# Attention units in a fused attention and mixture kernel: the softmax normalisation of one unit issued behind the maximum of the next

## The chip, the cores and the metric

The kernel runs on one core of a Trainium2 chip. The core has five engines that work side by side, each with its own queue in program order: TensorE (PE, matrix products; PEld is its loading of weights), VectorE (DVE), ScalarE (ACT), GpSimd (POOL) and SyncE (SP), whose queue issues the DMA transfers. Engines wait for one another through semaphores. The metric is the device time of one execution in microseconds, as a median of runs.

## What is computed

Three layers follow each other. The first is attention in chunks over 4 x 8 heads, 768 positions and 64 channels, the second a gated layer of 512 to 2048 to 512, the third eight dense experts weighted by a Sinkhorn balanced gate:

```python
scores = scale * np.matmul(q_c, k_full.transpose(0, 1, 3, 2))
scores = scores - np.max(scores, axis=-1, keepdims=True)
a = np.exp(scores)
a = a / (np.sum(a, axis=-1, keepdims=True) + 1e-09)
out[:, :, c_start:c_end] = np.matmul(a, v_full)
...
h = x @ w_in
g = h * np.clip(h + 3.0, 0.0, 6.0) / 6.0
x = g @ w_out
...
for e in range(E):
    h = np.maximum(x @ w1[e], 0.0)
    out += P[:, e:e + 1] * (h @ w2[e])
```

## The kernel before

Products run in three passes of TensorE: each operand is held as a high and a low part, and high x high, high x low and low x high are added up (`passes`, L230 to L232). ScalarE makes the high part by a copy (`hh`, `xh`), VectorE the low part by a subtraction (`hl`, `xl`).

The attention is cut into 32 units of 96 queries by 8 heads. A unit goes through these steps: its scores (`a_scores`, L286, one bank of PSUM for each half of the heads); the mask added while the scores are taken out of PSUM (L297), the maximum of each row and head (L305) and its negated, scaled copy `nm` (L310), all three on VectorE in `a_max`; eight exponentials on ScalarE, one for each head, which also sum the rows (`a_exp`, L322); the normalisation on VectorE in `a_norm`, with the tiny addition to the sum `sm` (L330), the reciprocal `rc` (L332) and the multiplication (L333); eight transposes on TensorE into `pt` (`a_turn`, L340) and two copies of these by ScalarE into `et` (`a_copy`, L168); and the product with the values, `av` (`a_values`, L360). Its result is split into parts `xh` and `xl`, and GpSimd adds these to `xf`, which is stored for the residual of later layers (`a_whole`, L384).

The second layer runs in the same loop over `steps`. A step makes one product of 128 hidden rows by 384 tokens (`layer_product`, 12 matmuls into `ph`), the bias and relu on ScalarE (L430, tile `t`), the gate's product on VectorE (L435), the two parts, and two steps later the second product into `pa` (`second`, 12 matmuls). From the 17th step on, every odd step ("due") carries the parts of three units: the values of unit u, the normalisation of unit u + 1, the scores, maximum and exponentials of unit u + 2. The even step behind it carries the transposes of unit u + 1. The code's order in a step is the order in each engine's queue: the kernel is written under a manual schedule. On ScalarE the order from one due step on is: exponentials of u + 2, relu of the even step, `et` copies of u + 1, then the next due step.

Beside this run two streams of work. Weights come as wide integers and are converted on ScalarE and VectorE (L148 to L161). And a "factory" on GpSimd makes sums and differences of expert weights for the third layer: 80 jobs, each a load, four additions (tile `fr`, L717) and a store, paced by the number of the step.

Of the kernel before, what the change touches and what calls it, by code (L numbers as in the profile page):

```python
# [67 lines left out]
def attn_moe_moe(ctx: ExitStack, tc: tile.TileContext, qk, vw, wi, wo, wa, wb, wg, out):  # L68
# [10 lines left out]
    def pool(name, bufs, space=None, side=None):  # L79
        kw = {} if space is None else {"space": space}  # L80
        if side:
            kw["side"] = side
        return tc.tile_pool(name=name, bufs=bufs, reuse_waits="tile", **kw)
# [40 lines left out]
    def w_load(f):  # L124
        for t in "ab":
            s = wst[1, f, t] = st_p.tile([128, DM], F32, tag=f"s{t}", name=f"s{t}")
            nc.sync.dma_start(out=s, in_=wd[t, f])
# [18 lines left out]
    def single_act(n):  # L146
        rest = at_p.tile([128, DM], U32, tag="rest", name="rest", bufs=3)
        nc.scalar.activation(out=rest, in_=words(n)[0], func=AF.Copy, scale=7.49 * 2.0 ** -32)  # L148
        pw = at_p.tile([128, DM], F32, tag="pw", name="pw", bufs=3)
        nc.scalar.activation(out=pw, in_=words(n)[1].bitcast(F32), func=AF.Abs, scale=2.0 ** -112)  # L150
        wst[n] = pw, rest
# [20 lines left out]
    def single_hi(n, eng=nc.scalar):  # L172

        pe, f, t = wide[n]
        if pe == 0:
            hi = w_p.tile([128, DM], F32R, tag=f"w{t}h", name=f"w{t}h")
            copy(hi, wst[n], eng)
            wts[t, pe, f] = hi
# [26 lines left out]
    def convert_act(n):  # L205

        for m in range(going[0], min(going[0] + n, len(wide))):
            single_act(m)
        for m in range(going[1], going[0]):
            single_hi(m)  # L210
        going[1] = going[0]
# [192 lines left out]
    def stage(do, u):  # L404
        if u < NU:
            do(u)
# [31 lines left out]
    def first(i):  # L438
        layer_product(i)
        layer_relu(i)  # L440
        layer_times(i)
# [32 lines left out]
    def spill():  # L474
        while spills:
            nc.sync.dma_start(out=spills[0][0], in_=spills.pop(0)[1])
# [375 lines left out]
    def w1_load(g):  # L852
        if g < NW:
            n, k, p = W1[g]
            e = n % NE
            s = w1s[g] = w1s_p.tile([128, 2, 256], F32, tag="w1s", name="w1s", bufs=4)
            wk = wa[4 * e:4 * e + 4].rearrange("k p (a f) -> p k a f", a=4)
            if k in FORM and p in (1, 2):
                for j in range(2):
                    nc.sync.dma_start(out=s[:, j].rearrange("p (k f) -> p k f", k=2),  # L860
                                      in_=quarter((ws3 if k == DEEP else ws4)[e], W3S[S1 + 2 * p - 2 + j]))
            elif k in FORM:
                q = wk[:, :, (A12 if k == DEEP else A22) + 1].rearrange("p k (j f) -> p j k f", j=2)
                for j in range(2 if p == 0 else 1):
                    nc.sync.dma_start(out=s[:, j].rearrange("p (k f) -> p k f", k=2),
                                      in_=q[:, j, :2] if p == 0 else q[:, 1, 2:])
            elif FIRST[p][0] < S1:
                nc.sync.dma_start(out=s, in_=wk[:, k:k + 2, FIRST[p][0] + 1])
            else:
                nc.sync.dma_start(out=s, in_=ws1[2 * e + k // 2][:, W1S[FIRST[p][0]]])  # L870
# [10 lines left out]
    def w1_hi(g):  # L881
        if g < NW:
            w1[g] = w1_p_tile("h")
            nc.scalar.activation(out=w1_part(g, w1[g]), in_=w1_part(g, w1s[g]), func=AF.Copy)  # L884

    def w1_lo(g):
        if g < NW and w1_low(g)[1]:
            lo = w1_p_tile("l")
            nc.vector.tensor_tensor(out=w1_part(g, lo), in0=w1_part(g, w1s.pop(g)),
                                    in1=w1_part(g, w1[g]).bitcast(F32), op=ALU.subtract)  # L890
            w1[g] = w1[g], lo
        elif g < NW:
            w1[g] = w1[g], w1l.pop(g)
# [13 lines left out]
    def w2_load(m):  # L907
        if m < 7 * NM:
            e, a = m // 7 % NE, SECOND[m % 7][0]
            s = w2s[m] = w2s_p.tile([128, 4, 256], F32, tag="w2s", name="w2s")  # L910
            if a >= S1:
                nc.sync.dma_start(out=s, in_=ws2[e][:, W2S[a]])
                return
            for g in range(2):
                of = wb[e, g].rearrange("p (c a d) -> p c a d", c=2, a=4)[:, :, {A11: 0, A12: 2, A22: 3}[a]]
                nc.sync.dma_start(out=s[:, 2 * g:2 * g + 2], in_=of)
# [242 lines left out]
    with tc.manual_schedule():  # L1159
# [10 lines left out]
        def rate(i):  # L1170

            pe, b, f = steps[i]
            return 0 if pe or b == NB1 - 1 else f % 2
# [6 lines left out]
        def sums_due(i):  # L1180
            now = i if i <= NB1 * NF else NB1 * NF + (i - NB1 * NF) * PACE
            for stage_, late in ((2, 2.6), (0, 0), (1, 1.3)):
                while begun[stage_] < len(jobs) and starts[begun[stage_]] + late <= now:
                    jobs[begun[stage_]][stage_]()
                    begun[stage_] += 1

        for i, (pe, b, f) in enumerate(steps):
            if i < 2 * NF:
                continue
            u, turn, due = (i - 2 * NF) // 2 + 3 * UPB, i % 2 == 0, i % 2 == 1  # L1190
            turn, due = (pe == 0 and w for w in (turn, due))
            if (pe, b, f) == (0, NB1 - 1, 0):
                at_ctx.__exit__(None, None, None)
            if (pe, b, f) == (1, 1, 0):
                three.close()
                xo_p = ctx.enter_context(pool("xo", 1, side="right"))
                xb_p = xb_ctx.enter_context(pool("xb", 1, side="right"))
            if (pe, b, f) == (1, NB2 - 1, 2):
                assert build is None and begun[2] == len(jobs)
                xb_ctx.close()  # L1200
                two.close()
                w1s_p, w1r_p, w2s_p = (
                    ctx.enter_context(pool(n, 1, side="right")) for n in ("w1s", "w1r", "w2s"))
                for g in range(4):
                    w1_load(g)
                w2_load(0)
            if (pe, b) == (1, NB2 - 1) and 3 <= f <= AHEAD + 2:
                w1_hi(f - 3)
                w1_lo(f - 3)
                if f < AHEAD + 2:  # L1210
                    w1_load(f + 1)

            sums_due(i)
            if pe == 0 and b == NB1 - 1:
                w_load(f)
                if f == 0:
                    x_load(0)
            if pe == 1 and f == 1 and b + 1 < NB2:
                x_load(b + 1)
            if pe == 1 and f == 5:  # L1220
                x2_load(b)
            ready = pe == 1 and f == 3 and later
            spill()
            first(i)
            if pe or due:
                first_parts(i)
            if due:
                stage(a_values, u)
                stage(a_split, u)
                stage(a_norm, u + 1)  # L1230
                stage(a_scores, u + 2)
                stage(a_max, u + 2)
                convert_act(rate(i))
                stage(v_load, u + 2)
            if ready:
                gate_logits(later[0])
                gate_copy(later[0])
            second(i - LAG)
            if ready:
                gate_turn(later.pop(0))  # L1240
            if pe:
                sums_due(i + 0.5)
            if due:
                stage(a_exp, u + 2)
                stage(a_load, u + 4)
            if pe == 0 and not due:
                if turn:
                    stage(a_transpose, u)
                first_parts(i)
                convert_act(rate(i))  # L1250
            if pe == 0:
                convert(rate(i))
            if pe == 0 and b == NB1 - 1 and f >= LAG:
                w_split(f - LAG)
            elif pe == 1 and b == 0 and f < LAG:
                w_split(NF - LAG + f)

            n = b + 1 if pe else 0
            r = f - 2 - pe
            if 0 <= r < KT and n < NB2 and (pe or b == NB1 - 1):  # L1260
                x_split(n, r)
            if (pe, b, f) == (1, 2, 6):
                build = x_ops(0, xb_p, "xb")
            if build:
                build = build if next(build, 0) is None else None
# [228 lines left out]
```

## Time and profile before

| | us |
|---|---|
| median of 3 runs (2518.59 to 2521.33) | 2519.56 |
| the profiled execution | 2521.98 |
| its span, first to last instruction | 2519.9 |
| TensorE busy in the span | 2484.1 (99%) |
| VectorE busy | 1995.3 (79%) |
| ScalarE busy | 1445.8 (57%) |
| GpSimd busy | 947.5 (38%) |

The due steps that the change touches lie between about 128 and 356 us of the span. The list of waits names a waiting engine and line, and the engine and line that ended the wait. A timeline row gives start, length, engine, line, and in brackets how long the engine had stood idle before it and what released it. Matmuls overlap: one that is listed with 0.34 us may begin 0.17 us behind the one before it.

### The profile page before, as it was taken

The numbers are of one execution on the slowest core, as the hardware profiler recorded it, in microseconds if no ns is written. First come the engines' busy times: TensorE is split into PE (matmuls) and PEld (weight loads), VectorE is DVE, ScalarE is ACT, GpSimd is POOL, SyncE is SP. The second block draws the span as 40 slices with busy tenths as digits, with TensorE's granted clock in tenths as the row PEclk, the third lists the DMA queues.
The fourth block names the chain that finished last, engine by engine and source line by source line (L and its number), as shares of the span: only waits on it lengthen the run. The fifth ranks groups of instructions, "written<-read, shape, count | busy, mean of one in ns | idle before, by whom it ended". The sixth has DMA issues, their size and how long they took to land. (4 is left out here: it accounts for less than half of the span.)

```text
span 2519.9 us, 37015 instructions
## 1 busy us (share of the span) xinstructions
PE 2484.1 (99%) x13092; PEld 2125.0 (84%) x13092; DVE 1995.3 (79%) x2440; ACT 1445.8 (57%) x2686; POOL 947.5 (38%) x705
## 2 busy tenths in 40 slices
PE   9989999999999999999999999999999999999999
PEld 8988889878778888888888888888888888888888
DVE  8777757567489999999997787778788677777777
ACT  8656654122265655565666655566666666656555
POOL 0154556666006535344533233333233222232231
PEclk9999999999999999999999999999999999999999
DMA  7679969887465676676768777667777667776664
GB/s 208 195 241 294 286 214 317 276 302 252 143 224 173 221 235 226 223 240 198 242 223 281 253 246 241 221 232 235 240 254 243 225 226 230 234 230 205 216 220 157
DMA packets 379990, 587.45 MB, mean 233 GB/s; under 512 B 30675, under 2 KB 229276, under 8 KB 379804
## 3 DMA queue, kind: packets, MB, share of 16 engines
q1 hardware_dynamic: 379520, 584.85, 71.3%
q8 instruction: 103, 1.69, 0.3%
q14 instruction: 83, 0.68, 0.1%
q10 hardware_dynamic: 284, 0.24, 0.0%
HBM read 444.36 MB, written 140.61 MB: 232 GB/s over the span
## 5 line engine op out<-in xcount | busy, mean ns | idle before, releaser
L1011 POOL TENSOR_TENSOR g<-g,pb 128x512 f32<-128x512 f32 x304 | 561.3, 1864 | 1183.1 <-ACT g L1004 849.8
L1062 ACT ACTIVATE oh<-g 128x1024 fp32r<-128x1024 f32 x336 | 355.1, 1057 | 358.9 <-PE oa L232 107.8
L1067 DVE TENSOR_TENSOR ol<-g,oh 128x1024 fp32r<-128x1024 f32 x336 | 458.7, 1367 | 52.5 <-ACT oh L1062 52.3
L717 POOL TENSOR_TENSOR fr<-fr 128x256 f32<-128x256 f32 x320 | 275.3, 861 | 180.4 <-DMA fr<-in_wa_dram 98.0
L230 PE MATMUL ga<-xo,w1h 128*128 128x512 f32 (+1 forms) x864 | 314.1, 364 | 2.0 <-ACT g L979 1.5
L232 PE MATMUL ga<-xo,w1l 128*128 128x512 f32 (+1 forms) x864 | 312.8, 362 | 0.0
L231 PE MATMUL ga<-xo,w1h 128*128 128x512 f32 (+1 forms) x864 | 312.6, 362 | 0.0
L1037 DVE TENSOR_TENSOR g<-g 128x1024 f32<-128x1024 f32 x192 | 306.6, 1635 | 0.0
L231 PE MATMUL oa<-ol,w2h 128*128 128x512 f32 x760 | 298.1, 392 | 0.0
L230 PE MATMUL oa<-oh,w2h 128*128 128x512 f32 x760 | 297.7, 392 | 0.0
L232 PE MATMUL oa<-oh,w2l 128*128 128x512 f32 x760 | 296.1, 390 | 0.0
L884 ACT ACTIVATE w1h<-w1s 128x512 fp32r<-128x512 f32 (+1 forms) x416 | 249.9, 601 | 41.4 <-issue 19.0
L996 DVE TENSOR_TENSOR g<-g,ga 128x512 f32<-128x512 f32 x192 | 130.6, 680 | 103.4 <-PE ga L232 103.4
L1004 ACT ACTIVATE g<-g 128x512 f32<-128x512 f32 x288 | 178.0, 619 | 42.0 <-DVE g L996 41.6
L230 PE MATMUL gc<-xo,w1h 128*128 128x512 f32 (+1 forms) x544 | 195.6, 360 | 1.7 <-ACT g L979 0.8
L430 ACT ACTIVATE t<-ph,half 128x384 f32<-128x384 f32 (+1 forms) x112 | 69.7, 622 | 219.5 <-PE ph L232 213.3
L232 PE MATMUL gc<-xo,w1l 128*128 128x512 f32 (+1 forms) x544 | 194.8, 358 | 0.0
L231 PE MATMUL gc<-xo,w1h 128*128 128x512 f32 (+1 forms) x544 | 194.6, 358 | 0.0
L921 ACT ACTIVATE w2h<-w2s 128x1024 fp32r<-128x1024 f32 x168 | 176.8, 1052 | 27.8 <-DMA w2s<-in_wb_dram 19.3
L230 PEld LDWEIGHTS ga<-xo,w1h 128*128 128x128 f32 x864 | 162.7, 188 | 34.9 <-ACT g L979 3.0
L231 PEld LDWEIGHTS ga<-xo,w1h 128*128 128x128 f32 x864 | 162.6, 188 | 28.5
L232 PEld LDWEIGHTS ga<-xo,w1l 128*128 128x128 f32 x864 | 162.5, 188 | 25.1
(195 smaller groups left out, 5685.3 us busy)
## 6 DMA issues: line engine op xcount, KB each, us to landing
w1l<-wl SPq DMA_DIRECT2D x232, 256.0 KB, 4.1
w2l<-wl SPq DMA_DIRECT2D x112, 512.0 KB, 3.8
w1s<-ws SPq DMA_DIRECT2D x192, 256.0 KB, 4.8
w2s<-ws SPq DMA_DIRECT2D x96, 512.0 KB, 5.0
ws<-fr SPq DMA_DIRECT2D x80, 512.0 KB, 5.1
w2s<-in_wb_dram SPq DMA_DIRECT2D x144, 256.0 KB, 3.6
wl<-w1l SPq DMA_DIRECT2D x128, 256.0 KB, 4.0
wl<-w2l SPq DMA_DIRECT2D x56, 512.0 KB, 4.2
```

Of the source, the lines that this page charges most:

```text
L230: nc.tensor.matmul(ps, wh, xh, start=start, stop=False, skip_group_check=more)
L231: nc.tensor.matmul(ps, wh, xl, start=False, stop=False, skip_group_check=more)
L232: nc.tensor.matmul(ps, wl, xh, start=False, stop=stop, skip_group_check=more)
L717: nc.gpsimd.tensor_tensor(out=o, in0=a, in1=b, op=f)
L884: nc.scalar.activation(out=w1_part(g, w1[g]), in_=w1_part(g, w1s[g]), func=AF.Copy)
L921: nc.scalar.activation(out=hi, in_=w2s[m], func=AF.Copy)
L996: nc.vector.tensor_tensor(out=g, in0=g, in1=ps, op=ALU.add)
L1004: nc.scalar.activation(out=g, in_=g, func=AF.Relu)
L1011: nc.gpsimd.tensor_tensor(out=g, in0=g, in1=p, op=ALU.mult)
L1037: nc.vector.tensor_tensor(out=o, in0=gq[n, x, i], in1=gq[n, y, i], op=ALU.subtract)
L1062: nc.scalar.activation(out=hi, in_=gq[n, b, i], func=AF.Copy)
L1067: nc.vector.tensor_tensor(out=lo, in0=gq[n, b, i], in1=op[m, i].bitcast(F32), op=ALU.subtract)
```

## The change

In a due step the normalisation of unit u + 1 is issued behind the scores and the maximum of unit u + 2, where it stood ahead of both:

```diff
             if due:
                 stage(a_values, u)
                 stage(a_split, u)
-                stage(a_norm, u + 1)
                 stage(a_scores, u + 2)
                 stage(a_max, u + 2)
+                stage(a_norm, u + 1)
                 convert_act(rate(i))
                 stage(v_load, u + 2)
```

`a_scores` issues only on TensorE, `a_norm` and `a_max` only on VectorE, so VectorE's queue alone changes its order. On VectorE, in a due step that also converts weights, the place reads as follows (`hl` is the low part of the second layer's hidden rows, `xl` that of the attention's result, `e` the scores and then the exponentials, `sa` a converted weight):

```order
 L452 TENSOR_TENSOR hl<-t,hh 128x384
 L378 TENSOR_TENSOR xl<-av,xh 128x4x96
-L330 TENSOR_SCALAR sm<-sm 96x8
-L332 RECIPROCAL rc<-sm 96x8
-L333 TENSOR_TENSOR e<-e,rc 96x1024
 L297 TENSOR_TENSOR e<-sc,mk 96x512 x2
 L305 TENSOR_REDUCE mx<-e 96x8
 L310 TENSOR_SCALAR nm<-mx 96x8
+L330 TENSOR_SCALAR sm<-sm 96x8
+L332 RECIPROCAL rc<-sm 96x8
+L333 TENSOR_TENSOR e<-e,rc 96x1024
 L159 SCALAR_TENSOR_TENSOR sa<-raw,rest 128x512
```

The three instructions of the normalisation moved behind the four of the mask and maximum; this occurs in 18 due steps, those of the units 12 to 29 with u as above. On TensorE the instructions keep their places, but the first transposes of a unit name other semaphores:

```order
 L231 MATMUL pa<-hl,wbh 128x384
 L232 MATMUL pa<-hh,wbl 128x384
-L340 MATMUL pt<-ident,e 128x96 [waits DVE_49]
+L340 MATMUL pt<-ident,e 128x96 [waits DVE_49,PE_49]
 L340 MATMUL pt<-ident,e 128x96 x3
-L340 MATMUL pt<-ident,e 128x96 [waits DVE_49]
+L340 MATMUL pt<-ident,e 128x96 [waits PE_49]
 L340 MATMUL pt<-ident,e 128x96 x3
 L230 MATMUL ph<-xh,wah 128x384
```

Before, the two halves waited on VectorE for the additions that empty the score banks; now the first waits for the normalisation, and both also name TensorE's own semaphore, for the scores that lay in these banks.

## Rows read from the trace of the kernel before

**Rows 1.** The page, busy time: engine, us, share of the span, instructions.

```profile
PE 2484.1 (99%) x13092; PEld 2125.0 (84%) x13092; DVE 1995.3 (79%) x2440; ACT 1445.8 (57%) x2686; POOL 947.5 (38%) x705
```

**Rows 2.** Waits of TensorE, whole span: waiter, releaser, total us, times, longest.

```profile
PE av L360 <- ACT et L168: 20.5, 18, 2.0
```

**Rows 3.** Waits of all engines from 130 to 370 us.

```profile
ACT e L322 <- DVE nm L310: 76.4, 18, 6.0
...
PE av L360 <- ACT et L168: 20.0, 16, 2.0
```

**Rows 4.** Timeline of one unit: start us, us, engine, line, operation.

```profile
205.87 0.99 PE L360 MATMUL av<-et,vw 128*64 128x96 f32 x16 [0.90 <-ACT et L168]
...
206.79 1.12 PE L286 MATMUL sc<-qk 64*96 64x128 f32 x16
...
208.93 0.16 DVE L330 TENSOR_SCALAR sm<-sm 96x8 f32<-96x8 f32 x1
...
209.36 1.22 DVE L333 TENSOR_TENSOR e<-e,rc 96x1024 f32<-96x1024 f32 x1
...
210.50 1.28 DVE L297 TENSOR_TENSOR e<-sc,mk 96x512 f32<-96x512 f32 x2
...
211.81 1.22 DVE L305 TENSOR_REDUCE mx<-e 96x8 f32<-96x1024 f32 x1
...
213.06 0.42 DVE L310 TENSOR_SCALAR nm<-mx 96x8 f32<-96x8 f32 x1
...
213.51 0.40 ACT L322 ACTIVATE e<-e,nm 96x128 f32<-96x128 f32 x1 [4.06 <-DVE nm L310]
...
214.02 0.81 PEld L340 LDWEIGHTS pt<-ident,e 96*128 96x128 f32 x8
...
216.61 0.56 ACT L430 ACTIVATE t<-ph,half 128x384 f32<-128x384 f32 x1
216.62 0.34 PE L231 MATMUL ph<-xl,wah 128*128 128x384 f32 x1
...
216.79 0.34 PE L232 MATMUL ph<-xh,wal 128*128 128x384 f32 x1
...
217.07 0.84 ACT L168 ACTIVATE et<-pt 128x384 f32<-128x384 f32 x2
...
217.86 0.98 PE L360 MATMUL av<-et,vw 128*64 128x96 f32 x16 [0.73 <-ACT et L168]
```

**Rows 5.** Single lines, 130 to 370 us: ns min/median/max, first and last start.

```profile
L310 DVE TENSOR_SCALAR nm<-mx x18: 167/585/743, 135.9 to 351.3; 96x8 f32<-96x8 f32 x18
L330 DVE TENSOR_SCALAR sm<-sm x19: 155/157/243, 131.1 to 359.3; 96x8 f32<-96x8 f32 x19
L305 DVE TENSOR_REDUCE mx<-e x18: 1215/1216/1218, 134.6 to 350.0; 96x8 f32<-96x1024 f32 x18
L333 DVE TENSOR_TENSOR e<-e,rc x19: 1220/1835/1848, 131.7 to 359.7; 96x1024 f32<-96x1024 f32 x19
L717 POOL TENSOR_TENSOR fr<-fr x122: 722/738/1727, 129.6 to 367.4; 128x256 f32<-128x256 f32 x122
```

**Rows 6.** Stretches: us, busy PE, PEld, DVE, ACT, POOL; clock, DMA share, GB/s.

```profile
193.71:205.87 12.16, 11.26 (x88) 10.67 (x89) 9.01 (x14) 7.30 (x27) 6.93 (x8) 1.00 1.09 336
280.14:283.95 3.81, 3.81 (x34) 3.31 (x34) 2.65 (x7) 2.96 (x7) 0.00 (x0) 0.55 1.09 370
370.00:390.00 20.00, 20.00 (x117) 20.00 (x116) 10.60 (x19) 9.91 (x23) 10.16 (x13) 1.00 1.03 360
130.00:370.00 240.00, 217.23 (x1656) 206.00 (x1656) 167.98 (x262) 140.11 (x470) 128.01 (x142) 0.99 0.83 259
```

**Rows 7.** Timeline of GpSimd and VectorE about 184 us.

```profile
184.14 1.03 POOL L384 TENSOR_TENSOR xf<-xh,xl 128x384 f32<-128x384 f32 x1 [2.57 <-DVE sm L330]
185.13 1.72 POOL L717 TENSOR_TENSOR fr<-fr 128x256 f32<-128x256 f32 x1
...
184.40 1.85 DVE L333 TENSOR_TENSOR e<-e,rc 96x1024 f32<-96x1024 f32 x1
```

## The prediction

> **What bounds the kernel now.** I read the shares of busy time first. TensorE (PE) is busy 2484.1 us of the 2519.9 us span, 99% [rows 1], so a change off its path is worth at most about the 36 us in which it stands still. The next view, who waits for whom on PE over the whole span, says where these are: 20.5 us in 18 waits are the values product `av` waiting for ScalarE's copies `et` [rows 2]. No other line of that list comes near it. The same list limited to the attention steps, 130 to 370 us, holds 20.0 us in 16 of these waits, and beside them the largest wait of all: ScalarE's exponentials wait 76.4 us for the negated maximum `nm` of VectorE, once in each of 18 units [rows 3].
>
> The timeline of one unit joins the two. Take the unit that begins with `av` at 205.87 [rows 4]. Its scores are finished on PE at 206.79 + 1.12 = 207.91. VectorE is free for them at 208.93, but first runs the normalisation of the other unit (208.93 to 210.50), then the two additions of the mask, the maximum and `nm` (213.06 to 213.48). ScalarE, idle for 4.06 us, begins the eight exponentials at 213.51, goes on without a pause to the bias-and-relu `t` at 216.61 and the two `et` copies from 217.07, and PE, idle for 0.73 us, begins the next `av` at 217.86. So `et` is late because it stands behind the exponentials in ScalarE's queue, these because `nm` is late, and `nm` because the normalisation goes first. The result of the normalisation isn't read before the transposes, whose first weight load comes at 214.02.
>
> **The change part by part.** No instruction is added or removed. In 18 units three VectorE instructions go from ahead of the two additions to behind `nm`. The queues of PE, ScalarE, GpSimd and SP keep their order, so no DMA moves in its queue; what VectorE does behind the group, the conversion of the weights, starts when it did, since the group holds the same work.
>
> *What `nm` gains.* The moved group lasts 210.50 - 208.93 = 1.57 us in this unit, where the multiplication took 1.22 us [rows 4], and up to 0.63 more where it took 1.85: its shortest is 1220 ns, its longest 1848 [rows 5]. The scores are there 1.02 us before VectorE turns to them, so the additions do start 1.57 us earlier, and the exponentials and `et` with them. The copies then run from 215.50 to 216.34 (0.84 us). PE's product before `av` issues its last matmuls at 216.62 and 216.79, 0.17 apart, so PE could begin `av` at 216.96; the copies are 0.6 us ahead of that. I cost every one of the 16 waits as gone. If `nm` is 0.6 us later than this, a wait begins to come back.
>
> *The sum.* 16 waits: 20.0 us [rows 3]. A wait also breaks the overlap of matmuls: 217.86 - 216.96 = 0.90 us were lost where the list counts 0.73, which is 0.17 more, an estimate of 16 x 0.15 = 2.4 us. The longest wait, 2.0 us, was followed by a stretch of 3.81 us with the clock granted at 0.55 on average, between the 1.2 and the 2.4 GHz level [rows 6]: 0.45 x 3.81 = 1.7 us, which go with the wait. Together 24.1 us.
>
> *What it adds.* The first transposes now wait for the end of a normalisation that comes later. In the unit shown, the additions and the maximum end at 208.93 + (213.06 - 210.50) = 211.49. With the shortest `nm` (0.17) and multiplication (1.22) the normalisation ends at 211.49 + 0.17 + 0.03 + (209.36 - 208.93) + 1.22 = 213.34, 0.7 us before the weight load at 214.02. With a usual `nm` (0.59) and the long multiplication (1.85) it ends at 214.39, late by 0.4. Behind the waiting load stand the next product and `av`, so all of it would be lost on PE. (The transposes also come to name PE's own semaphore, for the scores that lay in their bank; those ended at 207.91, so that costs nothing.)
>
> Which of the two holds is decided by GpSimd. The row of the slow multiplication, 184.40 to 186.25, stands beside a GpSimd addition `xf` that had begun at 184.14, and the `fr` behind that took 1.72 us [rows 7] against a median of 0.738 [rows 5]: one of the two stands still until the other has ended. The maximum (1215 to 1218 ns) is never touched [rows 5]. The Trainium skill, "SBUF — State Buffer", section "Who interferes with whom", states this as an exclusive lock: a VectorE instruction with two inputs in SBUF, or in a two-port mode, and a GpSimd instruction that reads SBUF shut each other out, whoever issues second waits to the end of the first, and a reduction never takes part. The trace agrees (1.85 against 1.22 us, and 1.22 always for the reduction). By that rule the change removes one collision (`xf` now starts beside the additions, which read PSUM) and sets the three locking instructions `nm`, `sm` and the multiplication into GpSimd's `fr` chain.
>
> GpSimd is busy 128.0 of 240 us here [rows 6], so I take 10 of the 18 units as late by 0.4: 4 us. Bounds: nothing, if the group always meets an idle GpSimd; and, if `sm` too waits for a whole `fr` of 0.74 us every time, 0.4 + 0.7 = 1.1 us in each of 18 units, 20 us. `sm` never took more than 0.243 us [rows 5], right behind another VectorE instruction as it will stand now, so I stay near the lower end.
>
> Net: 24.1 - 4 = 20.1 us. The profiled execution took 2521.98 us, so it would be 2501.9. It lies 2.4 us above the median of the runs, 2519.56, which I carry over: 2499.5 us. After the attention steps PE waits for almost nothing [rows 1, 2], so the saving should arrive at the end whole.
>
> **The rivals.**
>
> *The transposes take over the wait.* If VectorE loses its turn to GpSimd at `sm` also, most units pay 0.8 us: 18 x 0.8 = 14.4, net 9.7, 2510 us. For it: `nm` (167 to 743 ns) and the multiplication (1220 to 1848) vary by what GpSimd holds up [rows 5], and three such instructions come to stand in a row. Against it: the 0.243 us of `sm`. This is what the lock of "SBUF — State Buffer" in the Trainium skill would do at its worst.
>
> *Transfers set the pace.* Where the DMA engines are busy throughout, a unit can't shrink. The unit from 193.71 has a share of 1.09 at 336 GB/s [rows 6], the whole stretch one of 0.83 [rows 6]. If under half of the units are held in this way, 10 of the 22.4 us of waits come back as waits for a transfer: net 24.1 - 4 - 10 = 10.1, 2509.5 us. Against it: 370 to 390 us moves 360 GB/s with PE busy throughout [rows 6], and no wait of PE in these steps names a DMA.
>
> *Slower.* The transposes' wait grows until the clock falls. Let `nm`, `sm` and the multiplication each wait for GpSimd: 1.1 us a unit, 20 in all. Where such a wait nears the 2.0 us behind which the clock fell [rows 3, 6], 1.7 us follow; six such falls are 10.2 us. Then 24.1 - 20 - 10.2 = -6.1, 2525.7 us. It decides from 1.34 us a unit (24.1 / 18). Nothing in the trace shows a chain of three such losses.
>
> *The change doesn't do what it says.* If `nm` were held by something other than the normalisation, the time would stay at 2519.6. For it: nothing but that a wait is put down to the last releaser. Against it: the additions follow the normalisation without a gap in the timeline, 1.02 us of it after the scores were ready [rows 4].
>
> **How the numbers follow.** Forecast 0.73, transposes 0.13, transfers 0.08, slower 0.03, nothing 0.03. The forecast's own range is 2494 to 2506: no late transpose gives 2519.56 - 24.1 = 2495.5, with 1.5 us for the overlap term, which I know from one unit; one late by 0.6 in all 18 gives 10.8 us and 2506. The range 2494 to 2510 holds nearly all of the first (0.70) and reaches to the middle of the transposes' case and of the transfers (half of 0.21): about 0.8. A difference of 0.2%, 5 us, is about what a measurement of this kernel can tell from no change. Faster by more than that: the forecast, the transfers and most of the transposes' case, 0.92. Within: the rest of that and the last rival, 0.05. Slower: 0.03.
>
> **What would show it.** In the profile after, the waits of `av` for `et` should be gone from PE's list or under 2 us in all, and the exponentials' wait for `nm` should fall by about 18 x 1.6 = 29 us, to some 48. A unit should last about 11.3 us, its busy time on PE, instead of 12.2 [rows 6]. New on PE's list: transposes `pt` waiting for `e` of the multiplication, 2 to 8 us in all. The stretch at half clock near 280 us should be missing. I am wrong if `av` still waits for `et`, if `pt` waits for more than 10 us, or if units get shorter and a later step waits for a transfer instead.

## The result and the profile after

The changed kernel takes 2497.03 us (median of 5 runs, 2495.97 to 2498.95), against 2519.56 before on the same chip. The ratio is 0.9909 with a 95% interval of 0.9894 to 0.9923, that is 22.5 us faster. The forecast was 2499.5. A second timing on another chip gave 2498.10 against 2521.87, ratio 0.9906 (0.9889 to 0.9922).

The profiled execution took 2498.2 us with a span of 2496.2, 23.7 us shorter than the span before. The first thing to look at is again what TensorE waits for, over the whole span (waiter, releaser, total us, times, longest):

```profile
PE pa L230 <- DVE x L525: 2.1, 1, 2.1
...
PE pt L340 <- DVE e L333: 0.8, 4, 0.2
...
PE av L360 <- ACT et L168: 0.5, 2, 0.3
```

The 20.5 us of `av` waiting for `et` [rows 2] are down to 0.5. Three of the four waits at the transposes lie in the opening: between 130 and 350 us one of 0.2 us is left. In that stretch the exponentials still wait for `nm`, but half as long [rows 3]:

```profile
ACT e L322 <- DVE nm L310: 39.3, 18, 3.4
...
PE pt L340 <- DVE e L333: 0.2, 1, 0.2
```

The timeline of one unit answers to [rows 4]: start, length, engine, line, operation.

```profile
198.84 0.88 PE L360 MATMUL av<-et,vw 128*64 128x96 f32 x16
...
202.26 1.27 DVE L297 TENSOR_TENSOR e<-sc,mk 96x512 f32<-96x512 f32 x2
...
203.56 1.22 DVE L305 TENSOR_REDUCE mx<-e 96x8 f32<-96x1024 f32 x1
...
204.81 0.17 DVE L310 TENSOR_SCALAR nm<-mx 96x8 f32<-96x8 f32 x1
204.89 0.16 DVE L330 TENSOR_SCALAR sm<-sm 96x8 f32<-96x8 f32 x1
205.01 0.40 ACT L322 ACTIVATE e<-e,nm 96x128 f32<-96x128 f32 x1 [2.78 <-DVE nm L310]
205.32 1.22 DVE L333 TENSOR_TENSOR e<-e,rc 96x1024 f32<-96x1024 f32 x1
...
206.88 0.81 PEld L340 LDWEIGHTS pt<-ident,e 96*128 96x128 f32 x8
...
208.58 0.85 ACT L168 ACTIVATE et<-pt 128x384 f32<-128x384 f32 x2
...
209.93 0.88 PE L360 MATMUL av<-et,vw 128*64 128x96 f32 x16
```

Read it from both ends. `et` ends at 209.43, half a microsecond ahead of `av`, which carries no mark of an idle time. The multiplication ends at 206.54, 0.34 us ahead of the weight load that needs it. A unit takes 209.93 - 198.84 = 11.09 us, where it took 12.16 [rows 6]. Over the middle of the attention steps, before and then after, TensorE's idle time falls from 17 us of 190 to 0.2:

```profile
150.00:340.00 190.00, 173.06 (x1342) 164.06 (x1341) 137.37 (x212) 116.37 (x394) 102.30 (x114) 0.99 0.90 278
```

```profile
150.00:340.00 190.00, 189.80 (x1495) 179.98 (x1494) 148.91 (x232) 129.46 (x432) 111.74 (x125) 1.00 0.97 298
```

The columns are those of [rows 6]. The clock's mean is now 1.00: no stretch at half clock is left in it. The DMA engines moved 298 GB/s instead of 278 and nothing on TensorE waited for them. Single lines between 130 and 350 us (ns, min/median/max) answer to [rows 5]:

```profile
L310 DVE TENSOR_SCALAR nm<-mx x18: 167/168/358, 134.2 to 326.9; 96x8 f32<-96x8 f32 x18
L333 DVE TENSOR_TENSOR e<-e,rc x19: 1220/1222/1834, 134.7 to 335.9; 96x1024 f32<-96x1024 f32 x19
L330 DVE TENSOR_SCALAR sm<-sm x19: 153/160/1030, 134.2 to 335.4; 96x8 f32<-96x8 f32 x19
```

`nm` and the multiplication are held up less often than before (medians 168 and 1222 ns against 585 and 1835), while `sm`, never above 0.243 us before, took 1.03 us in one unit and 0.71 in another.

### The profile page after: what moved, and what is told of

It reads as the page before. It is cut to its first block, busy times and chain, and to the rows that moved or that the text cites. A ratio compares the mean times of both kernels' runs of the same rounds, so it can differ in the third digit from the quotient of the medians.

```text
span 2496.2 us, 37032 instructions
## 1 busy us (share of the span) xinstructions
PE 2480.8 (99%) x13092; PEld 2120.4 (85%) x13092; DVE 1986.4 (80%) x2440; ACT 1448.5 (58%) x2686; POOL 952.4 (38%) x705
## 5 line engine op out<-in xcount | busy, mean ns | idle before, releaser
L1011 POOL TENSOR_TENSOR g<-g,pb 128x512 f32<-128x512 f32 x304 | 572.3, 1900 | 1176.8 <-ACT g L1004 953.2
```

The source lines that it names most:

```text
L1011: nc.gpsimd.tensor_tensor(out=g, in0=g, in1=p, op=ALU.mult)
```

## The experiments

The theory to test: the loss ran along one chain, normalisation, `nm`, exponentials, `et`, `av`; it went because `nm` now comes earlier, by some 1.6 us if nothing holds the normalisation up, and it ends where `et` has slack before `av`. The rival grew out of the last rows above: `nm` and the multiplication are now held up less by GpSimd, and this, not the order, could have made the difference. The kernel before differs by some 3 us from chip to chip (2519.56 to 2522.57), so each run is compared with the kernel before on its own chip. Each run adds or moves work only.

**Collisions alone.** In the kernel before, GpSimd's `xf`, and with it its store, is issued one step later:

```diff
         a_high(u)
         a_low(u)
-        a_whole(u)
+        if u == NU - 1:
+            a_whole(u)
...
                 if turn:
                     stage(a_transpose, u)
+                    if 3 * UPB < u < NU:
+                        stage(a_whole, u - 1)
```

> The order of before, but GpSimd's addition xf is issued one step later, so that it no longer starts beside the normalisation's multiplication. Theory: about 10 of 18 units lose 0.6 us less on the way to nm, so the waits for et fall by 6 us at most and the time is 2513 to 2519 us. Rival (collisions made the whole difference): the time comes down to 2497 to 2500 us.

Measured: 2518.11 us against 2521.73, ratio 0.9982 (0.9973 to 0.9992), 3.6 us less. The multiplication's median came down as far as in the changed kernel, yet the waits for `et` stayed:

```profile
L333 DVE TENSOR_TENSOR e<-e,rc x19: 1220/1222/1842, 131.5 to 355.4; 96x1024 f32<-96x1024 f32 x19
```

```profile
PE av L360 <- ACT et L168: 18.7, 17, 1.8
```

But `nm` itself was held up nearly as much as before (median 585 ns in both):

```profile
L310 DVE TENSOR_SCALAR nm<-mx x18: 167/585/766, 135.4 to 346.8; 96x8 f32<-96x8 f32 x18
```

Added up over all units, `nm` and the multiplication took 13.7 us more than their shortest times in the kernel before, and 9.9 us more here. So the run takes away only part of the collisions, and 3.6 us is not a bound for all of them. What it shows is that the multiplication's are not the main cause; the rival is answered by the next run.

**ScalarE's queue alone.** VectorE's order is left as before; the exponentials are issued behind the two copies:

```diff
             if due:
-                stage(a_exp, u + 2)
                 stage(a_load, u + 4)
             if pe == 0 and not due:
                 if turn:
                     stage(a_transpose, u)
+                    if u + 1 >= 3 * UPB + 2:
+                        stage(a_exp, u + 1)
```

> The order of before on VectorE (normalisation ahead of the maximum), but ScalarE's exponentials of the next unit issued behind the two et copies of the even step instead of ahead of them. Theory (the queue of ScalarE carries the loss: et stands behind exponentials that wait for nm): the waits of av for et go although VectorE's order is that of before, TensorE runs units of about 11.1 us, and the time is 2497 to 2503 us. Rival (the gain came from fewer collisions of VectorE with GpSimd, in which the normalisation is held up): these stay as before, the time stays at 2517 to 2521 us.

Measured: 2507.66 us against 2521.73, ratio 0.9942 (0.9927 to 0.9957), 14.1 us less. The waits for `et` are gone from TensorE's list with the normalisation still ahead of `nm`, so the copies were late because they stood behind the exponentials. GpSimd still holds up `nm` and the multiplication here, by 11.0 us in all against 13.7 before, so the waits can go without fewer collisions. But the expected 2497 to 2503 was missed, since `av` has a new wait that the list puts down to nothing:

```profile
PE av L360 <- issue: 7.1, 11, 1.5
```

One such place of that run:

```profile
212.55 0.54 DVE L435 SCALAR_TENSOR_TENSOR t<-t,ph 128x384 f32<-128x384 f32 x1
...
213.19 0.88 PE L360 MATMUL av<-et,vw 128*64 128x96 f32 x16 [0.99 <-issue]
```

`av` takes one of the two PSUM banks that the products `ph` use, and starts 0.1 us behind the last reader of `ph` on VectorE. In the queue of VectorE that reader (L435) stands behind the late `nm`. That the 7.1 us are this bank's is read from the times of this place; no run takes the bank away.

**How much slack `et` has.** The changed kernel with a copy of the exponentials onto themselves behind the eight exponentials, so that ScalarE alone is later. Three sizes; the largest is

```diff
+        if u >= ADDED:
+            nc.scalar.activation(out=ef, in_=ef, func=AF.Copy)
+            nc.scalar.activation(out=ef, in_=ef, func=AF.Copy)
         if 1 in halves:
             e_t[u] = ef, sm
```

the middle one has one copy, the smallest one copy of half the heads (`ef[:, :4]`).

> The changed kernel with one more ScalarE instruction in each of the 18 units, behind the eight exponentials: a copy of 96x512 onto itself, an estimated 0.56 us from the 0.60 us of 128x512 copies. Only the et copies come later, no VectorE or GpSimd order changes. By the trace of the changed kernel et is done 0.5 to 1.09 us ahead of av, 0.85 on the mean. Theory (loss begins where the slack of et ends): 0 to 2 us, 2496 to 2499 us. Rival (collisions of VectorE with GpSimd made the gain, so ScalarE's order doesn't matter): 2495 to 2499 as well; this run tells only with the next two.

> The same with a copy of 96x1024, an estimated 1.0 us. Theory: the slack of 0.85 is used up, av waits about 0.3 us in most of 18 units and loses the overlap too: 4 to 9 us, 2501 to 2506 us. Rival (collisions): 2495 to 2499 us.

> The same with two copies of 96x1024, an estimated 2.0 us, which is 0.4 more than the normalisation took ahead of nm. Theory: av waits 1.2 to 1.4 us in each of 18 units, 22 to 28 us: 2519 to 2526 us, the time of before although the normalisation stands behind nm. Rival (collisions): 2495 to 2499 us.

| added on ScalarE | time, us | before on that chip | ratio (interval) | `av` waits for `et`, 126 to 375 us |
|---|---|---|---|---|
| nothing | 2497.03 | 2519.56 | 0.9909 (0.9894 to 0.9923) | none |
| half a copy, 0.62 us | 2499.65 | 2522.57 | 0.9909 (0.9894 to 0.9924) | none |
| one copy, 1.06 us | 2504.94 | 2522.57 | 0.9931 (0.9915 to 0.9948) | 4.0 us in 8 |
| two copies, 2.12 us | 2521.82 | 2522.57 | 0.9996 (0.9987 to 1.0006) | 22.4 us in 17 |

The rows of the two larger sizes (lines shift by the added ones):

```profile
PE av L362 <- ACT et L168: 4.0, 8, 0.8
```

```profile
PE av L363 <- ACT et L168: 22.4, 17, 1.8
```

Half a copy costs nothing that the ratio shows, one copy costs some 5 us, two copies bring back the whole time of before although the normalisation stands behind `nm`. The loss begins between the two smaller sizes, as the 0.5 to 1.1 us that `et` is ahead of `av` in the changed trace say. A lateness of ScalarE by itself makes the old kernel's time, with VectorE's and GpSimd's order as in the changed kernel.

**How much slack the transposes have.** The changed kernel with one more reduction on VectorE, behind `nm` and ahead of the normalisation:

```diff
+    def a_extra(u, n=NH):
+        ef = e_t[u][0]
+        x = sm_p.tile([UQ, NH], F32, tag="rc", name="xx")
+        nc.vector.tensor_reduce(out=x[:, :n], in_=ef[:, :n], axis=AX.X, op=ALU.max)
...
                 stage(a_max, u + 2)
+                if u + 2 < NU:
+                    a_extra(u + 1)
                 stage(a_norm, u + 1)
```

> The changed kernel with one more reduction of 96x1024 on VectorE (1.22 us, never held up by GpSimd) between nm and the normalisation. It moves the end of the normalisation, not nm. By the trace of the changed kernel the normalisation ends 0.15 to 1.06 us ahead of the transposes, 0.6 on the mean. Theory: the transposes then wait 0.7 us in each of 18 units and the overlap goes, together 12 to 17 us: 2509 to 2514 us, with the wait listed at pt for e of the multiplication. Rival (the transposes have far more room, and the forecast's term for them was a false fear): under 3 us, 2497 to 2500.

Measured: 2514.73 us against 2521.73, ratio 0.9968 (0.9955 to 0.9981). That is 0.0059 or some 15 us slower than the changed kernel, which is the expected 12 to 17 us (the time itself lies just above the range, as the kernel before is 2.2 us slower on this chip), and the wait is at the transposes:

```profile
PE pt L345 <- DVE e L333: 9.0, 14, 1.4
PE pa L230 <- ACT t L435: 3.6, 1, 3.6
```

The fear in the forecast was therefore real in kind: 1.2 us later, the normalisation does cost. (The 3.6 us lie in the first unit, where the four additions that are L525 in the changed kernel come later too; the list names `t`, which ended just before the wait did. That unit took 17.5 us instead of 15.0, so some 2.5 of the 15 us are not the transposes'.)

**A further version.** What is left in the changed kernel is the first unit's 2.1 us, where TensorE waits for additions (L525) that empty its banks and that stand behind the normalisation. The normalisation goes behind the second product in the code, which alters VectorE's order in this unit only:

```diff
                 stage(a_max, u + 2)
-                stage(a_norm, u + 1)
                 convert_act(rate(i))
...
             second(i - LAG)
+            if due:
+                stage(a_norm, u + 1)
```

> The changed kernel with the normalisation issued one call later in the code, behind the second product: VectorE's order differs in one unit only, the first, where four additions that empty banks of PSUM (L525) now go ahead of the normalisation. TensorE waits 2.11 us there for the first of these, and then runs at half clock for some us. If that wait is due to the normalisation being ahead: 1.9 us of it go, and up to 1.8 us of half clock, 2493.5 to 2495.5 us. Rival (the additions wait for TensorE's products instead, or the transposes behind then wait for the normalisation): 2496 to 2498 us.

Measured: 2496.13 us against 2521.73, ratio 0.9894 (0.9879 to 0.9908). The time is above the expected 2493.5 to 2495.5 and just within the rival's range, but the kernel before is 2.2 us slower on this chip, and the ratio is 0.0015 or some 4 us below the 0.9909 of the changed kernel on another. So both were timed again on one chip.

> The changed kernel once more, as it is, on the same chip as the next run, so that the two can be compared. By its first timing 0.9909 of before, 2494 to 2501 us.

> The normalisation behind the second product, once more, beside the changed kernel. Theory: its profile shows the wait of 2.11 us and the half clock behind it replaced by one wait of 1.16 us at the transposes, so 1.5 to 3.5 us less than the changed kernel of the same chip. Rival (the saving is given back later, or lies within the scatter of chips): within 1 us of it.

Measured there: the changed kernel 2498.10 (2496.05 to 2498.29), ratio 0.9906 (0.9889 to 0.9922); the further version 2495.77 (2493.93 to 2496.21), ratio 0.9895 (0.9880 to 0.9909). That is 2.3 us less. The intervals of the ratios overlap, and so do the ranges of the single runs, by 0.2 us, so the size is uncertain. Between 126 and 350 us one line of waits is left on TensorE, in the first trace of this version and in the second:

```profile
PE pt L340 <- DVE e L333: 1.3, 2, 1.2
```

```profile
PE pt L340 <- DVE e L333: 0.6, 1, 0.6
```

It has the lowest ratio of the kernels run: the wait for L525 is exchanged for a shorter one at the transposes. Part of the 2.3 us may be the clock: all eight executions of this version have a mean granted clock of 1.000, while six of the nine of the changed kernel have 0.999. On the chip that timed both, the changed kernel took 2496.05 us in its one execution at 1.000 and 2498.06 to 2498.29 in the three at 0.999.

## Why the prediction was right, point by point

*The chain.* `et` late behind the exponentials, these behind `nm`, `nm` behind the normalisation. Moving the exponentials alone takes the waits for `et` away, delaying ScalarE alone brings them back, and taking away about half of the multiplication's collisions leaves them (18.7 of 20.0 us). The order of VectorE is the one thing that the change itself moves. Yet `nm` gained more than the 1.57 us that the forecast took for a normalisation that nothing holds up: leaving out the first unit, it ended on the mean 8.09 us behind the start of `av` before and 5.80 after, 2.29 earlier. The other 0.7 us are what collisions cost in a unit before (13.7 us in 18): those of the multiplication, which no longer stands ahead of `nm`, and those of `nm` itself. The 1.57 us of the order are more than the 1.25 us of the mean wait (20.0 in 16), so the order could do without them; what the collisions alone are worth, no run here shows.

*The gain.* The sum forecast 20.0 us of waits, 2.4 of lost overlap and 1.7 of half clock, 24.1 us. The profiled span fell by 23.7. Between the `av` of the second unit and the last `av` it took 222.80 us before and 199.21 after, 23.6 less; with 20.0 of waits and 1.7 of half clock gone and 0.7 newly lost at the transposes (below), 2.6 us are left for the overlap. So this term stands up: a unit takes 11.09 us, less than the 11.26 for which TensorE was busy in a unit before [rows 6], which is why the forecast "about 11.3" for a unit was too long. The exponentials' wait fell by 37 us, not by 29, as `nm` came 2.29 us earlier and not 1.6: the forecast had taken the normalisation without its collisions. The fall from 2519.56 to 2497.03 in the medians is 22.5, about 1 us less than between the two spans: the profiled execution lay 2.4 us above its median before, which the forecast carried over, and 1.2 after.

*The transposes.* This is the term that was mis-sized: "I take 10 of the 18 units as late by 0.4: 4 us". The list after has 0.2 us of it within the attention steps, that of the second timing 0.8 in two waits. With the overlap that is lost there too it is 0.7 and 1.2 us, by the units that last longer than the usual 11.09 us (11.25, 11.47 and 11.23 in the first trace). I had taken ten late units; three came late. In 11 of the 18 units at least one of the three instructions took more than its undisturbed time (7 multiplications, 5 `nm`, 2 `sm`), together 4.8 us, 0.43 in each of the 11. I had added the usual hold-up of `nm` and the longest of the multiplication in the same unit, 1.05 us, and that is what it takes to be 0.4 late. With 0.43 the normalisation still ends ahead of the weight load in most units, as one that nothing holds up ends 0.34 to 0.88 us ahead of it (the forecast had 0.7). My reason for staying near the lower end was that `sm` would not lose its turn. That was wrong: it lost its turn to GpSimd in two units of this trace, and in four of the second timing's for 1.01 to 1.03 us each:

```profile
215.50 0.17 DVE L310 TENSOR_SCALAR nm<-mx 96x8 f32<-96x8 f32 x1
215.56 1.03 POOL L384 TENSOR_TENSOR xf<-xh,xl 128x384 f32<-128x384 f32 x1
215.58 1.03 DVE L330 TENSOR_SCALAR sm<-sm 96x8 f32<-96x8 f32 x1
```

`sm` was issued 0.02 us behind `xf` and ended with it. The rule of "SBUF — State Buffer" in the Trainium skill (section "Who interferes with whom"), that the second to issue waits for the first, is what these rows show. That it cost so little is due to the slack ahead of the weight load and not to the forecast's reason. Nor did `xf` always start beside the additions, as the forecast had it: it did in 5 of the 18 units, and in five others it ran beside `nm` or `sm`.

*Transfers.* Not so: 298 GB/s instead of 278, share 0.97 instead of 0.90, and no wait of TensorE in these steps for a transfer.

*The rest of the kernel.* The saving arrived whole. From the last `av` (366.39 us before, 342.62 after) to the end it is 2153.5 and 2153.6 us.

## What to carry to other kernels

Where an engine at 99% waits a little in every round, follow the late operand through the queues of the engines ahead of it: here the time was lost two queues away, by VectorE doing first what was needed last. Before moving work back, measure both slacks, of what becomes earlier and of what becomes later; here `et` was late by 1.25 us on the mean and the normalisation ahead took 1.57 or more, while the transposes had about 0.6 to give (1.2 us added, 0.6 waited in each of 14 units). And when the main path is freed, look at what bounds the next unit: the version with the exponentials moved on ScalarE removed the same wait and got 14 of 22 us, since a second wait stood right behind it.

## What had not been expected

GpSimd and VectorE held each other up about as often after the change, but at other places: `hl` (L452) took over 0.06 us more than its shortest time in 20 of 36 instructions where it had in 2 of 34, and in the unit at 149 us `xf` took 2.00 us, and the conversion beside it 1.50, where 1.02 and 0.68 are usual.

```profile
149.63 2.00 POOL L384 TENSOR_TENSOR xf<-xh,xl 128x384 f32<-128x384 f32 x1
```

```profile
150.67 1.50 DVE L159 SCALAR_TENSOR_TENSOR sa<-raw,rest 128x512 uint32<-128x512 uint32 x1
```

TensorE's list shows no wait for either there, so these hold-ups cost nothing.

The clock did not fall behind each wait of the first unit: in the changed kernel's first profile the wait of 2.1 us was followed by a stretch at a mean of 0.67, in the second one of 1.8 us was not. The stretch of the first, then the wait and the stretch of the second:

```profile
136.00:140.00 4.00, 3.19 (x12) 3.23 (x13) 3.81 (x8) 2.02 (x10) 0.78 (x1) 0.67 0.16 14
```

```profile
PE pa L230 <- DVE x L525: 1.8, 1, 1.8
```

```profile
136.00:138.00 2.00, 2.00 (x14) 1.97 (x14) 1.90 (x4) 0.80 (x3) 0.00 (x0) 1.00 0.03 8
```

With at least 1.3 us lost in the first, this is more than half of the 2.1 us by which the two profiled spans differ (2496.2 and 2494.1). The length of the wait alone does not decide it: with the exponentials moved, TensorE waited 3.1 us at the same place, and the clock stayed at 1.00 behind it:

```profile
PE pa L230 <- DVE x L525: 3.1, 1, 3.1
```

```profile
138.00:140.00 2.00, 2.00 (x13) 1.97 (x13) 1.90 (x5) 0.00 (x0) 0.00 (x0) 1.00 0.03 8
```

What does decide it stays open.
